# Scores of a tile held back until the first-layer product of the tile four places before it is placed, with the order drawn anew

## The chip, the cores and the metric

The kernel runs on one core of a Trainium2 chip. The metric is the time of one execution in device microseconds (us). The core has a matrix engine (PE), a vector engine (DVE), an activation engine (ACT), a general engine (POOL), and a sync engine (SP) that issues all DMAs of this kernel. Each engine works through its own list of instructions in order; an instruction waits until the semaphores it names are reached, and everything behind it on the same engine waits with it.

## The reference, cut to what matters

Attention with pooled keys and values, then two feed-forward layers over its output:

```python
k_p = k.reshape(B, H, Sp, 8, D).mean(axis=3)       # B, H, S, D = 8, 8, 576, 64; Sp = 72
v_p = v.reshape(B, H, Sp, 8, D).mean(axis=3)
scores = q @ k_p.T / sqrt(D)
attn = softmax(scores)                             # over the 72 pooled keys
x = (attn @ v_p) as (4608, 512)
h = x @ w_in                                       # 512 -> 1024
solu = h * softmax(h)
ln = layernorm(solu) * g_ln
y = ln @ w_out                                     # 1024 -> 512
h2 = y @ w2_in                                     # 512 -> 2048
out = (h2 * sigmoid(1.702 * h2)) @ w2_out          # 2048 -> 512
```

## The kernel before, in words

The program has two parts. The first, up to about 450 us, computes attention and the first feed-forward layer and also prepares the weights of the second layer. The second, up to the end, is the second layer, written out by hand (lines 1300 to 1700). The change touches the first part alone.

The 4608 tokens are 36 tiles of 128, and every tile goes through one strand of steps (`attention`, line 854):

- its scores on PE (buffer `psx`, one bank pair for all tiles), taken from the transposed query `qt` and the pooled keys `kbd`;
- maximum and difference on DVE (`mx`, `e`), exponent on ACT, sum on DVE (`rs`), division on POOL (`e<-e,rs`), then a split into two 16-bit halves on ACT and POOL (`st`);
- a DMA transpose on SP (`aT<-st`), from tile 4 on issued for two tiles together;
- the values product on PE (buffer `psv`, a single one; `aT` with `vst`), which ACT and DVE copy out as `xT`.

A second strand (`hidden`) does the first-layer product of the tile on PE: 24 matmuls into `psh` (two buffers) from `xT` and the weights `w1i`, then maximum (`hmx`) and the softmax-times-h (`tt`) on DVE with an exponent on ACT (`he`). `hid[t]` is set when the plan gives the tile its `psh` buffer, before its matmuls are placed. A third strand per pair of tiles (`norm`) normalises on POOL and ACT (`zs`), transposes by DMA (`zT<-zs`), and starts two halves of the second matrix (`project`): each is 2 x 24 matmuls into `psy` (a single buffer) from `zT` and `w1o`.

Other strands pool keys and values of the eight batches (`half` to `kp`, `vp`; for batches 1 and 2 with matmuls into `psy`), and bring in and split the weights (`raw`, `w_f`, `hi`, `lo`). Each scale of a weight or of the values needs the largest value over all partitions: a matmul of `diag` with `ones` into `psy` (early) or `psv` (later), read by DVE (`w1o_all`, `w2all`, `v_all`). Until DVE has read it, that buffer is taken.

The order is made at build time by `Plan` (line 198). It keeps a list of strands, estimates for the next step of each when it could start, adds a term for its due time and a random number (`DRAWS`: up to a time of the plan's own clock, a size, a seed), and emits the step with the lowest score. What comes out is a fixed list for every engine. A lambda that a strand yields is a condition on the plan: the strand offers no further step until it holds. It puts no semaphore into the program; it only moves what is emitted. In the order rows, a name such as `psx_1467` is a buffer with the running number it got in that build, so numbers differ between the two kernels.

Of the kernel before, what the change touches and what calls it, by code (L numbers as in the profile page):

```python
# [78 lines left out]
DNS = 7  # L79
SG = 4  # L80
LAST = 90000
LATE = 3000
LATE_TURN = 3000
TTS = 4
DRAWS = ((70e3, 600, 13), (200e3, 150, 4), (330e3, 150, 13), (1e9, 150, 1))
V_TOP = 2.0 ** 14

TOP3 = 2.0 ** -29 * (1 - 2.0 ** -23)
# [95 lines left out]
class Plan:  # L184
# [7 lines left out]
    def __init__(self):  # L192
        self.free = dict.fromkeys(("pe", "dve", "act", "pool", "sp", "dma", "none"), 0.0)
        self.uses, self.floor, self.rings, self.ring_of = {}, {}, {}, {}
        self.strands, self.now, self.warm, self.pool_from = [], None, 0.0, 0.0
        self.draws = [(until, size, random.Random(seed)) for until, size, seed in DRAWS]

    def start(self, steps, due):
        s = Strand(self, steps, due)
        self.strands.append(s)  # L200
        return s
# [42 lines left out]
    def take(self, op, t, engine):  # L244
        if engine == "sp":
            begin = max(self.free["dma"], t + (1275 if op.turn else 1100))
            self.free["dma"] = end = begin + op.cost["sp"]
            self.free["sp"] = max(t + 625, end - 920) if op.turn else t + 520
            end += LATE_TURN if op.turn else LATE
            engine = "dma"  # L250
# [46 lines left out]
def moe_kernel(ctx: ExitStack, tc: tile.TileContext, qT, kT, vT, w_in, w_out, g_ln, w2_in, w2_out, eye, outT):  # L297
# [138 lines left out]
    with ExitStack() as ph:  # L436
# [22 lines left out]
        def until(*strands):  # L459
            return lambda: all(s.ended for s in strands)  # L460

        def there(*ins):

            return Op(("none",), lambda engine: None, [], ins, {"none": 0})
# [296 lines left out]
        def spans(t):  # L761

            b0, s0 = divmod(t * P, S)
            n = min(P, S - s0)
            parts = [(0, n, b0)]
            if n < P:
                parts.append((n, P - n, b0 + 1))
            return parts
# [88 lines left out]
        def attention(t):  # L857
# [5 lines left out]
            if t < 2:  # L863
                tiles[t].due = max(due(t) + LAG_ATT, DUE_ATT + STEP_ATT * t)
            yield lambda: all(k_ready[b] for _, _, b in spans(t)) and (t == 0 or scored[t - 1])
            e = yield New(sb, [P, H, SP], F32, "e", bufs=2)
            yield there(qt, *(kbd[b % 2] for _, _, b in spans(t)))
            ps = yield New(psx, [P, 2, 512], F32, "psx", "psx")
# [211 lines left out]

        EARLY, LATE = (slice(0, 2), slice(3, 6)), (slice(2, NS, 4),)

        class Quarter:
# [22 lines left out]
            def run(self, due):  # L1106
# [22 lines left out]
                def combine(slot, a, b, how):  # L1129
                    return VG("tensor_tensor", out=w[:, slot], in0=w[:, a], in1=w[:, b], op=how)  # L1130
# [4 lines left out]
                def split(slots):  # L1135
                    for s in slots:
                        yield A(out=hi[:, s], in_=w[:, s], func=AF.Copy)
                    for s in slots:
                        yield VG("tensor_tensor", out=lo[:, s], in0=w[:, s], in1=hi[:, s], op=ALU.subtract)
# [5 lines left out]
                yield combine(6, 1, 5, ALU.subtract)  # L1145
                second = start(split(LATE), due)
                yield until(first, second)
# [16 lines left out]
        def factors():  # L1164
            yield until(*units)
            cw, top = s1("cw", NU), s1("top")
            yield V(
                "scalar_tensor_tensor", out=co, in0=w1o_dn, scalar=1.0 / LN_UP, in1=g_dn, op0=ALU.mult, op1=ALU.mult
            )
            yield V("tensor_scalar_mul", ch, w2i_dn, co)  # L1170
            yield V("tensor_mul", cw, ch, w2o_dn)
            yield V("tensor_reduce", out=top, in_=cw, axis=AX.X, op=ALU.max)
            yield V("tensor_scalar_mul", co, top, 1.0 / G_DOWN)
            yield V("reciprocal", top, co)
            yield V("tensor_scalar_mul", gu, w2o_dn, top)

        def prepare_second():
# [46 lines left out]
            ytmp.release()  # L1224
            start(first_unit(), due(NTILE) + LAST)
            yield lambda: pairs[-1].normed
# [3 lines left out]
        def first_unit():  # L1230

            def product(p, bank, again=False):
                rows = [
                    (bank, w2i[0][:, w, A_OF[p], k], tok.ys[:, i, B_OF[p], k], False, k == 1 and w == 1)
                    for k in range(2)
                    for w, i in PASSES
                ]
                if again:
                    return T([(*r, True) for r in rows])
                return T([(*rows[0][:3], True, False)] + rows[1:])  # L1240

            def snap(i, bank):
                return A(out=first_c[:, i], in_=bank, func=AF.Copy)

            def add(i, bank):
                return V("tensor_tensor", out=first_c[:, i], in0=bank, in1=first_c[:, i], op=ALU.add)

            yield lambda: scored[NTILE - 1] and hid[NTILE - 1]
            banks = []
            for pool, name, bufs in ((psx, "psx", 1), (psh, "psh", 2), (psh, "psh", 2)):  # L1250
                banks.append((yield New(pool, [P, 2, 512], F32, name, name, bufs)))
            a, b, d = (x[:, 0, :TH] for x in banks)
            yield product(1, a)
            yield snap(Q11, a)
            yield product(2, b)
            yield add(Q11, b)
            yield product(6, a, True)
            yield snap(Q12, a)
            yield product(3, b)
            yield add(Q12, b)  # L1260
            yield product(7, a, True)
            yield snap(Q22, a)
            yield product(5, d)
            yield add(Q22, d)
            yield add(Q12, d)
            yield product(4, a, True)
            yield snap(Q21, a)
            drop(*banks)
# [3 lines left out]
        q_loaded, scored, turned, valued, hid = ([False] * NTILE for _ in range(5))  # L1272
# [21 lines left out]
        def due(t):  # L1294
            return FIRST_STEP + STEP * t
# [12 lines left out]
        user(keys(0, DUE_K0), DUE_K0)  # L1308
        user(eye_load(), DUE_W_IN + 1e3)
        tiles = [start(attention(t), DUE_Q + 100 * t) for t in range(2)]  # L1310
        am_in = s1("w1i_am", KM)
        w_in_done = user(w_in_scale(), DUE_SCALE)
# [4 lines left out]
        for b in range(1, B):  # L1317
            d = due(b * S // P + LEAD_KV) if b > 1 else DUE_KV1
            user(keys(b, d), d)
            user(values(b, d), d)  # L1320
        tiles += [start(attention(t), max(due(t) + LAG_ATT, DUE_ATT + STEP_ATT * t)) for t in range(2, NTILE)]
        pairs = [Pair(i) for i in range(NTILE // 2)]
        for p in pairs:
# [22 lines left out]
        factors_done = start(factors(), due(NTILE))  # L1346
        start(prepare_second(), due(NTILE) + LAST)
        plan.run()
# [381 lines left out]
```

## Time and profile before

| | us |
|---|---|
| median of 3 runs | 1172.87 |
| lowest, highest | 1170.4, 1172.99 |
| profiled execution, time | 1172.71 |
| profiled execution, span of its instructions | 1170.8 |
| PE busy | 1123.7 (96%) |
| ACT, DVE, POOL busy | 753.6, 727.7, 616.9 |

The profile is of one execution. Busy time of an engine counts its arithmetic instructions; the span runs from the first instruction to the last. A row of the timeline gives the start in us from the start of the span, the length, the engine, line and operation, what is written from what, and in brackets the idle time of the engine just before with the engine and buffer that ended it. PEclk is the granted clock of PE as a share of its full 2.4 GHz.

### The profile page before, as it was taken

What the parts mean: (1) busy time and instruction counts of PE and PEld (TensorE: products, weight loads), DVE (VectorE), ACT (ScalarE), POOL (GpSimd) and SP (SyncE); (2) the same over time, 40 slices, a digit from 0 to 9 for tenths busy, and PEclk for the clock granted to TensorE, in tenths of its full rate; (3) what the DMA queues carried; (4) which work ended last, traced back from release to release, by engine and by line L of the source; (5) the groups of instructions that cost most, each with busy time, mean ns of one, the idle gap of its engine ahead of it and who ended that gap; (6) DMA issues with size and microseconds to landing.
All of it is one profiled execution on the core that took longest, in us unless ns stands there. A gap on an engine that the chain in (4) does not pass through costs nothing.

```text
span 1170.8 us, 19698 instructions
## 1 busy us (share of the span) xinstructions
PE 1123.7 (96%) x7737; PEld 724.8 (62%) x7737; DVE 727.7 (62%) x1106; ACT 753.6 (64%) x997; POOL 616.9 (53%) x643
## 2 busy tenths in 40 slices
PE   4878999999999999999999999999999999999998
PEld 3545666667676667775566666666665665566665
DVE  7998888777677753337653774567266636753650
ACT  6888997988898784647624762674367337624740
POOL 4466999989999885325503530461056016503530
PEclk9999999999999999999999999999999999999999
DMA  9969999999999679255465355536453653463131
GB/s 366 276 179 286 226 274 286 285 260 247 287 272 216 162 181 268 74 174 235 138 197 183 127 165 163 190 125 203 141 174 126 214 167 137 147 203 117 60 120 60
DMA packets 247356, 225.75 MB, mean 193 GB/s; under 512 B 165728, under 2 KB 218080, under 8 KB 246752
## 3 DMA queue, kind: packets, MB, share of 16 engines
q1 hardware_dynamic: 247264, 224.50, 66.4%
q8 instruction: 60, 0.98, 0.3%
q14 instruction: 32, 0.26, 0.1%
HBM read 151.06 MB, written 33.55 MB: 158 GB/s over the span
## 4 chain that ended last, share of the span: by engine, by line
PE 70%; POOL 14%; ACT 7%; DVE 5%; issue 3%; DMA 1%; SPq 0%; POOLq 0%; ACTq 0%; DVEq 0%
PE bank_a L1386 32%; PE bank_d L1386 16%; PE bank_b L1386 8%; PE psy L537 6%; PE psh L537 6%; POOL w_f L496 4%; POOL lo L496 3%; PE psv L537 2%; POOL zs L496 2%; POOL st L496 2%; POOL e L496 1%; POOL q L496 1%; PE psx L537 1%; ACT st L496 1%; ACT tt L496 1%
## 5 line engine op out<-in xcount | busy, mean ns | idle before, releaser
L1386 PEld LDWEIGHTS <-w2o 128*128 128x128 f16 x2016 | 197.0, 98 | 130.4
L1386 PEld LDWEIGHTS <-w2i 128*128 128x128 f16 x1974 | 193.1, 98 | 128.4 <-issue 1.0
L349 POOL TENSOR_TENSOR w_g<-w_g 128x384 f32<-128x384 f32 x42 | 45.9, 1093 | 397.6 <-ACT w_g L1465 397.6
L1480 DVE SCALAR_TENSOR_TENSOR g<-w_g,gu_b,g 128x1152 f16<-128x1152 f32 (+1 forms) x96 | 175.9, 1833 | 87.1 <-ACT g L1475 86.8
L537 PE MATMUL psh<-w1i,xT 128*128 128x512 f16 x864 | 200.7, 383 | 5.5 <-ACT xT L496 3.8
L1386 PE MATMUL bank_a<-ys,w2i 128*128 128x384 f16 x1128 | 205.3, 326 | 0.0
L1386 PE MATMUL bank_a<-g,w2o 128*128 128x384 f16 x1152 | 201.6, 326 | 0.0
L537 PEld LDWEIGHTS <-w1o 128*128 128x128 f16 x1728 | 168.9, 98 | 32.1 <-DMA zT<-zs 2.9
L537 PE MATMUL psy<-zT,w1o 128*128 128x256 f16 x1536 | 177.9, 274 | 3.8 <-DMA zT<-zs 2.4
L1475 ACT ACTIVATE g<-w_g,gu_b 128x1152 f16<-128x1152 f32 (+1 forms) x96 | 134.1, 1409 | 48.5 <-POOL w_g L352 37.6
L1405 ACT ACTIVATE c<-bank_a 128x384 f32<-128x384 f32 x188 | 90.6, 482 | 102.3 <-PE bank_a L1386 101.8
L537 PEld LDWEIGHTS <-xT 128*128 128x128 f16 x864 | 82.9, 98 | 97.5 <-issue 4.9
L1386 PE MATMUL bank_d<-g,w2o 128*128 128x384 f16 x576 | 104.2, 326 | 0.0
L496 POOL TENSOR_TENSOR zs<-tt,zs 128x1024 f16<-128x1024 f32 x36 | 78.4, 2177 | 43.7 <-ACT zs L496 43.3
L1386 PE MATMUL bank_d<-ys,w2i 128*128 128x384 f16 x564 | 101.1, 326 | 0.0
L1465 ACT ACTIVATE w_g<-c,ch_b 128x1536 f32<-128x1536 f32 x47 | 73.7, 1568 | 28.3 <-DVE c L1408 28.3
L352 POOL TENSOR_TENSOR w_g<-w_g 128x384 f32<-128x384 f32 x42 | 82.5, 1963 | 0.0
L1408 DVE SCALAR_TENSOR_TENSOR c<-bank_d,c 128x384 f32<-128x384 f32 x94 | 51.9, 552 | 44.2 <-ACT c L1405 29.5
L496 POOL TENSOR_TENSOR lo<-w_f,hi 128x512 f16<-128x512 f32 (+1 forms) x48 | 64.8, 1369 | 6.8 <-DMA w2i_dram<-lo 5.2
L496 DVE TENSOR_REDUCE hmx<-psh 128x1 f32<-128x1024 f32 x36 | 43.8, 1218 | 35.1 <-PE psh L537 34.9
L537 PE MATMUL psx<-kbd,qt 128*128 128x144 f32 (+1 forms) x320 | 46.2, 306 | 13.9 <-ACT kbd L496 9.8
L496 DVE CUSTOM_DVE_ANT_0 tt<-psh,he 128x1024 f32<-128x1024 f32 x36 | 43.8, 1217 | 23.7 <-ACT he L496 21.8
(205 smaller groups left out, 1606.7 us busy)
## 6 DMA issues: line engine op xcount, KB each, us to landing
w2i<-w2i_dram SPq DMA_DIRECT2D x48, 896.0 KB, 4.5
w2o<-w2o_dram SPq DMA_DIRECT2D x84, 512.0 KB, 3.7
half<-kT SPq DMA_DIRECT2D x16, 576.0 KB, 6.3
half<-vT SPq DMA_DIRECT2D x16, 576.0 KB, 5.9
qt<-qT SPq DMA_DIRECT2D x36, 256.0 KB, 4.2
y_dram<-y SPq DMA_DIRECT2D x36, 256.0 KB, 3.5
y<-y_dram SPq DMA_DIRECT2D x48, 192.0 KB, 4.1
raw<-w_in SPq DMA_DIRECT2D x16, 512.0 KB, 7.8
```

Of the source, the lines that this page charges most:

```text
L349: eng.tensor_tensor(out=w[:, 1], in0=q[:, Q12], in1=q[:, Q11], op=ALU.subtract)
L352: eng.tensor_tensor(out=w[:, 3], in0=q[:, Q21], in1=w[:, 2], op=ALU.subtract)
L496: getattr(eng, name)(*args, **kw)
L537: nc.tensor.matmul(*p[:3], start=p[3], stop=p[4], skip_group_check=len(p) > 5)
L1386: nc.tensor.matmul(bank, self.weight(p, kk, w), self.data(p, kk, i), start=(first and kk == 0 and w == 0 and i == 0), stop=(last and kk == ...
L1405: nc.scalar.activation(out=self.c[:, i], in_=getattr(self, bank), func=AF.Copy, scale=self.scale)
L1408: nc.vector.scalar_tensor_tensor(out=self.c[:, i], in0=getattr(self, bank), scalar=self.scale, in1=self.c[:, i], op0=ALU.mult, op1=ALU.add,)
L1465: nc.scalar.activation(out=self.w[:, 0:4], in_=self.c, func=AF.Gelu_apprx_sigmoid, scale=self.ch)
L1475: nc.scalar.activation(out=self.g[s.start][:, 0], in_=self.w[:, s], func=AF.Copy, scale=self.gu)
L1480: nc.vector.scalar_tensor_tensor(out=self.g[s.start][:, 1], in0=self.w[:, s], scalar=self.gu, in1=self.g[s.start][:, 0], op0=ALU.mult, op1 ...
```

## The change

Two things change. A condition is put ahead of the scores of a tile: from tile 4 on, they are not offered to the plan until the first-layer product of the tile four places back has its buffer (`AHEAD_TO = 99` lies beyond the last tile, so the condition holds for all). And the table of random draws is another one: three stretches in place of four, with other seeds and other ends. Both move instructions in the lists of all engines in the first part; no operation of the reference is added or dropped. Between the engines that can each do a step, a few steps change place: PE has the same 14,804 rows, with 48 `project` matmuls in `psy` that were in `psv`; 8 exponents of one tile go to ACT, head by head.

```diff
 LAST = 90000
+AHEAD = 4
+AHEAD_TO = 99
 LATE = 3000
 LATE_TURN = 3000
 TTS = 4
-DRAWS = ((70e3, 600, 13), (200e3, 150, 4), (330e3, 150, 13), (1e9, 150, 1))
+DRAWS = ((70000.0, 600, 3), (360000.0, 150, 3), (1000000000.0, 150, 174017))
...
             yield lambda: all(k_ready[b] for _, _, b in spans(t)) and (t == 0 or scored[t - 1])
+            yield lambda: t < AHEAD or hid[t - AHEAD] or t >= AHEAD_TO
             e = yield New(sb, [P, H, SP], F32, "e", bufs=2)
```

SP, the stretch where the first normalised pair (`zs`, `zT`) meets the first loads of `w2_in` (`raw`). Before:

```order
42 L528 DMA raw_896<-w2_in 128x4x256 x2
43 L528 DMA raw_897<-w2_in 128x4x256 x2
44 L528 DMA raw_894<-w2_in 128x4x256 x2
45 L528 DMA qt_966<-qT 128x512
46 L528 DMA raw_895<-w2_in 128x4x256 x2
47 L528 DMA_TRANSPOSE zT_862<-zs_887 128x16x128
48 L528 DMA_TRANSPOSE zT_862<-zs_951 128x16x128
49 L528 DMA_TRANSPOSE aT_958<-st0_135 128x16x128
50 L528 DMA_TRANSPOSE aT_1053<-st1_136 128x16x128
```

The same stretch of SP now:

```order
42 L530 DMA raw_879<-w2_in 128x4x256 x2
43 L530 DMA half_877<-kT 128x1152
44 L530 DMA raw_942<-w2_in 128x4x256 x2
45 L530 DMA_TRANSPOSE zT_868<-zs_870 128x16x128
46 L530 DMA_TRANSPOSE zT_868<-zs_899 128x16x128
47 L530 DMA qt_1008<-qT 128x512
48 L530 DMA raw_940<-w2_in 128x4x256 x2
49 L530 DMA raw_941<-w2_in 128x4x256 x2
50 L530 DMA_TRANSPOSE aT_1000<-st0_135 128x16x128
51 L530 DMA_TRANSPOSE aT_1053<-st1_136 128x16x128
```

The two transposes of the first pair stood behind four pairs of `w2_in` loads and stand behind two; the transposes of tiles 6 and 7 (`aT`) stay behind all four.

DVE, around the values products of tiles 6 and 7 (`xT<-psv`). Before:

```order
171 L496 TENSOR_REDUCE w2a1_147<-w2am_146 128x1
172 L496 SCALAR_TENSOR_TENSOR xT_1234<-psv_1204,xT_1234 128x512
173 L496 TENSOR_REDUCE mx_1251<-psx_1246 128x8
174 L496 TENSOR_TENSOR e_1245<-psx_1246,mx_1251 128x576
175 L496 ISA tt_1275,mean_955<-psh_1047,he_1176 128x1024
176 L496 ISA mean_955 128x1
177 L496 SCALAR_TENSOR_TENSOR xT_1271<-psv_1238,xT_1271 128x512
```

Now:

```order
171 L498 TENSOR_REDUCE w2am_146<-raw_941 128x1
172 L498 TENSOR_REDUCE w2am_146<-raw_942 128x1
173 L498 TENSOR_REDUCE w2all_145<-psv_1222 128x1
174 L498 TENSOR_SCALAR w2all_145<-w2all_145 128x1
175 L498 ISA tt_1221,mean_951<-psh_1032,he_1212 128x1024
176 L498 ISA mean_951 128x1
177 L498 SCALAR_TENSOR_TENSOR xT_1244<-psv_1227,xT_1244 128x512
```

A scale product (`w2all`) now uses `psv` just ahead of tile 6, and DVE reads it behind two measurements of loaded weights. On PE the scores of tile 10 stood between the two values products; now the two stand next to each other.

PE, the scores of tile 12. Before:

```order
884 L537 MATMUL psh_1317<-w1i0_127,xT_1271 128x512
885 L537 MATMUL psx_1467<-kbd0_133,qt_1252 128x144 x4
886 L537 LDWEIGHTS xT_1271
887 L537 MATMUL psh_1317<-w1i0_127,xT_1271 128x512
888 L537 LDWEIGHTS xT_1271
```

Now:

```order
1067 L539 LDWEIGHTS vst0_131
1068 L539 MATMUL psv_1602<-aT_1286,vst0_131 64x128
1069 L539 MATMUL psx_1611<-kbd0_133,qt_1298 128x144 x4
1070 L539 LDWEIGHTS xT_1564
1071 L539 MATMUL psh_1609<-w1i0_127,xT_1564 128x512
```

They stood inside the first-layer product of tile 7 (`psh_1317`) and now stand right ahead of that of tile 8 (`psh_1609`), the tile four places back. In the other direction, the values products of tiles 12 to 15 come earlier: that of tile 12 stood behind the first-layer product of tile 11 and now stands inside that of tile 10.

## Rows read from the trace of the kernel before

**Rows 1.** Windows: length, busy us by engine, clock, DMA share, GB/s.

```profile
0.00:112.00 112.00, 80.27 (x562) 56.53 (x564) 94.91 (x179) 89.05 (x128) 62.42 (x73) 0.95 0.93 277
112.00:420.00 308.00, 297.31 (x2434) 207.49 (x2429) 233.72 (x433) 269.21 (x397) 286.02 (x340) 1.00 1.02 248
```

**Rows 2.** Waits of PE: buffer, releaser, total us, times, longest.

```profile
PE psv L537 <- DVE xT L496: 7.2, 8, 2.0
PE psy L537 <- ACT kp L496: 5.3, 2, 2.9
```

**Rows 3.** Timeline of PE, first values and first-layer products.

```profile
30.05 0.64 PE L537 MATMUL psv<-aT,vst 128*64 128x128 f16 x16
...
35.70 2.74 PE L537 MATMUL psh<-w1i,xT 128*128 128x512 f16 x6 [3.83 <-ACT xT L496]
```

**Rows 4.** Timeline of PE, two scale products at 70 us.

```profile
70.30 0.22 PE L537 MATMUL psy<-diag,ones 128*128 128x128 bf16 x1 [2.85 <-ACT kp L496]
72.54 0.22 PE L537 MATMUL psy<-diag,ones 128*128 128x128 bf16 x1 [2.03 <-DVE mean L496]
```

**Rows 5.** Timeline of PE, tiles 4 to 7 and first project half.

```profile
84.45 0.69 PE L537 MATMUL psv<-aT,vst 128*64 128x64 f16 x32
85.08 1.25 PE L537 MATMUL psx<-kbd,qt 128*128 128x144 f32 x8
87.57 0.64 PE L537 MATMUL psv<-aT,vst 128*64 128x128 f16 x16 [1.24 <-DVE xT L496]
88.14 5.35 PE L537 MATMUL psh<-w1i,xT 128*128 128x512 f16 x24
...
102.63 7.08 PE L537 MATMUL psy<-zT,w1o 128*128 128x256 f16 x48 [2.37 <-DMA zT<-zs]
109.64 0.64 PE L537 MATMUL psv<-aT,vst 128*64 128x128 f16 x16
...
111.69 0.64 PE L537 MATMUL psv<-aT,vst 128*64 128x128 f16 x16 [0.23 <-DVE xT L496]
```

**Rows 6.** Windows around the wait for zT.

```profile
99.90:103.40 3.50, 1.13 (x9) 0.70 (x8) 3.47 (x11) 3.48 (x6) 1.15 (x1) 1.00 1.04 232
103.40:106.80 3.40, 3.40 (x18) 2.35 (x16) 3.20 (x9) 3.37 (x5) 2.35 (x2) 0.50 1.21 222
```

**Rows 7.** Timeline of SP, w2_in loads and transposes.

```profile
80.80 5.28 SPq L528 DMA_DIRECT2D raw<-w_in  x6
...
90.78 9.57 SPq L528 DMA_TRANSPOSE zT<-zs  x2
```

**Rows 8.** Timeline of POOL, second tile of the first pair.

```profile
90.00 2.14 POOL L496 TENSOR_TENSOR zs<-tt,zs 128x1024 f16<-128x1024 f32 x1 [1.30 <-ACT zs L496]
```

**Rows 9.** Timeline of PE, later waits for psv.

```profile
187.87 0.70 PE L537 MATMUL psv<-aT,vst 128*64 128x64 f16 x32 [1.10 <-DVE xT L496]
...
206.74 0.64 PE L537 MATMUL psv<-aT,vst 128*64 128x128 f16 x16 [1.25 <-DVE v_all L496]
...
305.34 0.69 PE L537 MATMUL psv<-aT,vst 128*64 128x64 f16 x32 [2.10 <-DVE w2all L496]
...
401.68 0.69 PE L537 MATMUL psv<-aT,vst 128*64 128x64 f16 x32 [1.96 <-DVE xT L496]
```

**Rows 10.** Timeline of PE, project and scores in the steady stretch.

```profile
118.49 2.78 PE L537 MATMUL psy<-zT,w1o 128*128 128x256 f16 x24
...
126.32 1.14 PE L537 MATMUL psx<-kbd,qt 128*128 128x144 f32 x8
```

**Rows 11.** Timeline of POOL, end of tiles 8 and 34.

```profile
108.67 1.29 POOL L496 TENSOR_TENSOR st<-e,st 128x576 f16<-128x576 f32 x1
...
425.55 1.27 POOL L496 TENSOR_TENSOR st<-e,st 128x576 f16<-128x576 f32 x1
```

**Rows 12.** Transposes aT on SP from 90 to 420 us.

```profile
DMA to landing us min/median/max: 3.8/5.0/11.1
```

**Rows 13.** Timeline of PE, scores of tile 34.

```profile
402.31 1.25 PE L537 MATMUL psx<-kbd,qt 128*128 128x144 f32 x8
```

## The prediction

> **What bounds the kernel now.** I read the windows first, then the waits of PE, then its timeline at each long wait, and last the engines that ended those waits. In the steady stretch PE is busy 297.3 of 308 us, and POOL 286.0 of 308 [rows 1]. PE does the same products in either order, so all that a new order can give is PE's idle time: 112 - 80.3 = 31.7 us in the first 112 us, 308 - 297.3 = 10.7 us in the steady stretch, and some 1.7 us where PE ran at half its clock behind a wait (below). The hand-written second part, from about 510 us, keeps its lists in substance; I cost it at nothing.
>
> The idle time ahead of 112 us is mostly filling: the first keys, the first weights. In the steady stretch the reader is to see that PE waits hardly anywhere but at `psv`, the single buffer that a values product needs and that DVE has to read out first: 7.2 us over 8 waits for `xT`, some of them early, and the long single ones at 187.87, 206.74, 305.34 and 401.68 us [rows 2, 9]. So the question is which hand-overs of `psv` and `psy` get more PE work between them, which get less, and whether the held-back scores make the attention of a tile late.
>
> **The change part by part.** The sum goes against the profiled execution, 1172.71 us (span 1170.8 and 1.9 around it; the median of the runs is 1172.87).
>
> Start. The first values product ran at 30.05 us and the first-layer product at 35.70, after 3.83 us of idle time that ACT's copy of `xT` ended [rows 3]. Now the scale of `w_in` comes earlier in the lists, since its product no longer stands behind the 16 pooling matmuls of batch 1, but the transpose of tile 0 comes later, since POOL does two weight multiplications ahead of it instead of one, and 8 more pooling matmuls move into the gap. I take 0; at best the whole 3.8 us go, at worst the later transpose costs 3.
>
> The scales near 70 us. Two products of `diag` wait in turn for ACT's copy of `kp` (2.85 us) and for DVE (2.03 us), both because `psy` is taken [rows 4]. The first of the two, of `g_ln`, is now emitted earlier; but right behind the other, of `w_out`, stand four pooling matmuls that want `psy` again and so wait for the same DVE reading. I take 0, bounds 0 and -2.0.
>
> Tiles 4 and 5. Between their values products stood the scores of tile 8, and PE still waited 1.24 us [rows 5]. They now follow each other at once: the wait becomes 87.57 - (84.45 + 0.69) = 2.4 us, and the scores are done later. +1.2 us, bounds 0 and +1.3.
>
> First projection. PE waited 2.37 us for `zT`, and its clock then stood at 0.50 (1.2 GHz) from 103.4 to 106.8 us; the 48 matmuls took 7.08 us, where two runs of 24 later take 2.62 each from start to start, 118.49 to 121.11, the row of 24 itself 2.78 with its overlap [rows 5, 6, 10]. The transposes of this pair held SP for 9.57 us from 90.78, though POOL was done with the second tile at 92.14: they were queued behind four pairs of `w2_in` loads [rows 7, 8]. Now they stand ahead of two of these four, and ACT and POOL come to the second `zs` some 3 us earlier, counting the work ahead of it. The data can be there near 96 us, PE arrives at about 100.3. So the wait goes, 2.4 us, and the slow clock with it, 7.08 - 2 x 2.7 = 1.7 us: -4.1 us, bounds 0 and -4.1.
>
> By the Trainium skill, page "TensorE: Matmul & The Clock Gate", section "HAM oscillation — how this bites in real kernels", a wait for data in front of a product lets the clock fall, so that the product starts cold each time. The trace agrees at 102.63 us, with 0.50 behind 2.37 us of waiting, but not at 305.34, where 2.10 us of waiting left the clock at 1.00 in the window of the steady stretch [rows 1, 6, 9]. If each new wait of the list below cost a cold start like that one, the sum would be some 2 to 5 us higher.
>
> Tiles 6 and 7. Behind that projection a scale product now takes `psv` immediately ahead of tile 6, and DVE reads it only behind two measurements of `raw` weights, the last of the four loads. And tile 7 follows tile 6 with nothing between, where the scores of tile 10 hid all but 0.23 us of a hand-over of 111.69 - (109.64 + 0.57) = 1.5 us [rows 5]. I take 1.2 for the first and 1.2 more for the second, +2.4 us; bounds 0 and +5, the upper one if the last load is late.
>
> The steady stretch. Of the long waits, those for tile 13 (1.10 us), 14 (1.25), 22 (2.10) and 31 (1.96) have now 24 to 72 more project or first-layer matmuls ahead of them; what is late on DVE there hides behind these, 2.6 us and more [rows 9, 10]. -6.4 us, bounds -10.7 (all idle time of the stretch) and 0. New thin places: tiles 11 and 19 follow 10 and 18 with 6 first-layer matmuls between, 1.3 us against a hand-over of 1.5; tiles 16 and 17 lie closer; a scale product stands just ahead of tiles 10, 18, 26 and 30; and a 1.3 us stretch lies between two projections that share `psy`. With half a microsecond to one each, +4.0 us, bounds 0 and +14 (seven places with the longest wait seen, 2.1).
>
> The condition itself adds no wait on the chip. It shortens the stretch between scores and values product: counted on PE from the lists, from 35 to 56 us (tiles 8 to 35) to 28 to 49. What has to fit in: scores to the end of `st`, 109.96 - 85.08 = 24.9 us for tile 8 and 426.82 - 402.31 = 24.5 for tile 34 (first and last of 27 tiles, from 14 to 46, middle 22) [rows 5, 11, 13]; then the transpose, 5.0 us in the middle, 11.1 at most [rows 12]. That is 27 in the middle. Tile 12 is the tightest: between its scores and its values product now stand 60 first-layer matmuls (2.5 x 5.35), 96 project matmuls (4 x 2.62), three scores (3.4) and little else, 28 us [rows 5, 10]. I have put 1 us of lateness for it into the +4.0.
>
> Sum: 0 + 0 + 1.2 - 4.1 + 2.4 - 6.4 + 4.0 = -2.9 us, or 1169.8. DVE and ACT, which carry the moved steps, are idle for 74 and 39 us of the steady stretch [rows 1]; that is the cover of all that I cost at nothing, and where it fails, a wait of 1 to 2 us appears.
>
> **The rivals.**
>
> *The attention comes late (slower).* If scores to `st` keeps taking as long as for the slower tiles, 25.8 us (the value that three of the 27 exceed) and more with POOL at 93%, and the transpose takes 7, a values product needs 33 us. Tiles 12, 15, 24, 33 and 34 leave 28 to 31. They lie at three places; each would cost 3 to 4 us, +10.5 in all, and PE waits at `psv` for the DMA of `aT`. It decides from 28 us on. For it: POOL's rows in line, transposes held up by bulk loads [rows 7, 12]. Against it: the earlier scores just waited longer for buffers, so part of the 22 us was queueing behind other tiles. 1169.8 + 10.5 = 1180.
>
> *Nothing gained.* The projection's gain of 4.1 stays, but thin hand-overs cost all that the removed waits give, 6.4, and tiles 4 to 7 cost 3.6: 1172.2. For it: DVE's list sets these waits, and it is about as busy in any order.
>
> *More gained.* The plan sees hand-overs of `psy` and `psv` and places the reading on DVE right behind; then the thin places cost only 1 us in place of 4.0, and tiles 4 to 7 cost 1.6 in place of 3.6. 1172.7 - 4.1 - 6.4 + 1 + 1.6 = 1164.8. For it: 8 of the waits of `psv` average under 1 us [rows 2].
>
> *The condition does nothing* by itself, the redraw all: the plan would already hold scores back by its buffers. From tile 12 on, scores are placed 2 to 15 us of PE work later than before, so it acts; I keep it out of the chances.
>
> **How the numbers follow.** My forecast has 0.36 (1166 to 1173), late attention 0.21, nothing gained 0.19, more gained 0.24. About 0.3%, 3.5 us, is what a measurement of this kernel tells from no change. The forecast lies 2.9 us below, so it falls to faster by 0.16, to same by 0.18 and to slower by 0.02; nothing gained gives 0.15 to same, 0.04 to slower; late attention goes to slower, more gained to faster. Faster 0.40, same 0.33, slower 0.27. The range takes in the better half of the late attention and most of what more could be gained: 1162 to 1178.
>
> **What would show it.** In the profile after: no wait for `zT` at the first projection and a clock of 1.00 from 100 to 110 us; waits of 2 us and of over 1 us for `psv` at tiles 5 and 7, near 87 and 108 us; the wait near 70 us still there; in the steady stretch other tiles waiting at `psv`, ended by DVE, of some 8 us in all (10.7 idle now, less 6.4, plus 4.0). A wait for the DMA `aT<-st` at a values product of 2 us or more, above all at tiles 12, 24 or 33, would prove the forecast wrong and the first rival right; an idle time of PE ahead of 112 us that differs by over 4 us from 31.7 would put the cause in the start, which I costed at nothing.

## The result, and the profile after

The changed kernel takes 1183.95 us in the median of 6 runs (1181.85 to 1187.27), the kernel before on the same chip 1172.82 us (1170.03 to 1175.31): a ratio of 1.0107, with a 95% interval of 1.0090 to 1.0124. It is slower by 11.1 us between the medians and by some 12.5 us by the ratio, where 2.9 us less were forecast, and it lies above the range. The profiled execution took 1182.62 us, its span is 1180.8 us, 10.0 us longer than before.

The windows of the kernel after, with the columns of [rows 1] (length, then busy us of PE, PEld, DVE, ACT, POOL, the clock, the DMA share, GB/s):

```profile
0.00:112.00 112.00, 78.26 (x564) 55.33 (x565) 96.42 (x190) 91.60 (x132) 67.26 (x79) 0.95 0.99 274
112.00:420.00 308.00, 294.20 (x2359) 202.59 (x2358) 220.69 (x409) 263.15 (x386) 277.95 (x331) 0.98 1.04 245
```

PE idles for 33.7 us ahead of 112 us (31.7 before) and for 13.8 us in the steady stretch (10.7 before), and in that stretch its mean clock is 0.98 in place of 1.00. Busy time hides what a slow clock costs, so I set the two traces side by side at equal work: the work ahead of a matmul, each kind of matmul counted at its spacing at full clock, is taken from the time at which the matmul starts. What is left is all that PE has lost until then, in us:

| PE work done | before | after | difference |
|---|---|---|---|
| 88 | 41.1 | 41.8 | +0.7 |
| 96 | 41.7 | 49.2 | +7.5 |
| 184 | 46.6 | 49.8 | +3.2 |
| 240 | 47.6 | 60.8 | +13.2 |
| 352 | 53.3 | 60.8 | +7.5 |
| 432 | 53.7 | 61.2 | +7.5 |
| 464 | 55.3 | 65.3 | +10.0 |

So the front (to some 130 us of time) comes out even. Between the jumps the order before loses more than the new one, by 4.3 us from 96 to 184 and by 5.7 from 240 to 352; the four waits that were to go lie in these stretches. Three jumps, called hits from here on, take 6.8, 10.0 and 2.5 us. The first two are in the waits of PE from 112 to 450 us (buffer, releaser, total us, times, longest), which answer to [rows 2]:

```profile
PE psv L539 <- DMA half<-kT: 4.3, 1, 4.3
PE psh L539 <- DVE mean L498: 3.6, 1, 3.6
PE psy L539 <- ACT y L498: 2.3, 4, 1.3
PE psv L539 <- DVE xT L498: 2.0, 1, 2.0
PE psv L539 <- DVE v_all L498: 1.5, 1, 1.5
```

The first hit is at tile 8. PE's timeline (start, duration, in brackets the idle time ahead and its releaser), and DVE's of the same stretch:

```profile
129.50 0.22 PE L539 MATMUL psv<-diag,ones 128*128 128x128 bf16 x1
129.77 2.56 PE L539 MATMUL psy<-zT,w1o 128*128 128x256 f16 x22
136.67 1.06 PE L539 MATMUL psv<-aT,vst 128*64 128x128 f16 x16 [4.33 <-DMA half<-kT]
137.66 5.20 PE L539 MATMUL psy<-zT,w1o 128*128 128x256 f16 x24
```

```profile
129.89 1.23 DVE L498 CUSTOM_DVE_ANT_0 tt<-psh,he 128x1024 f32<-128x1024 f32 x1 [2.51 <-ACT he L498]
...
133.82 1.22 DVE L498 TENSOR_REDUCE w2am<-raw 128x1 f32<-128x1024 f32 x1 [2.50 <-DMA raw<-w_in]
134.95 1.22 DVE L498 TENSOR_REDUCE hmx<-psh 128x1 f32<-128x1024 f32 x1
...
136.33 0.28 DVE L498 TENSOR_REDUCE w2all<-psv 128x1 f32<-128x128 f32 x1
```

The page names the transfer `half<-kT` as what ended PE's wait, but nothing that the values product needs comes from there. DVE's row does: `psv` held a scale product, and its reader `w2all` ended at 136.33 + 0.28 = 136.61. The product was there at 129.72, but its reader stood in DVE's list behind `w2am`, which waited for its load until 133.82, and behind `hmx`. Behind the wait 24 project matmuls took 5.20 us in place of 2.62.

The second hit is a group of four waits from 256 to 296 us, on PE; then DVE ahead of the last of them, and SP ahead of that:

```profile
257.51 0.64 PE L539 MATMUL psv<-aT,vst 128*64 128x128 f16 x16 [1.47 <-DVE v_all L498]
...
272.71 2.78 PE L539 MATMUL psy<-zT,w1o 128*128 128x256 f16 x24 [1.27 <-ACT y L498]
...
287.26 0.64 PE L539 MATMUL psv<-aT,vst 128*64 128x128 f16 x16 [2.00 <-DVE xT L498]
...
295.21 7.03 PE L539 MATMUL psh<-w1i,xT 128*128 128x512 f16 x24 [3.64 <-DVE mean L498]
```

```profile
292.57 1.35 DVE L498 TENSOR_REDUCE kp<-half 128x144 f32<-128x1152 f32 x1 [5.25 <-DMA half<-kT]
293.84 1.22 DVE L498 CUSTOM_DVE_ANT_0 tt<-psh,he 128x1024 f32<-128x1024 f32 x1
```

```profile
274.77 9.84 SPq L530 DMA_TRANSPOSE zT<-zs  x2
...
286.79 0.41 SPq L530 DMA_DIRECT2D half<-kT  x1
```

The load left SP at 286.79, behind a pair of transposes that had held SP for 9.84 us, and landed at 292.57; the reader that frees `psh` (`tt`) stood behind its reader. The third hit is at 510.38, on PE and ahead of it on ACT, which comes to `c_kept` only behind `ys` and a table load:

```profile
510.38 1.24 PE L539 MATMUL psx<-ys,w2i 128*128 128x384 f16 x6 [2.09 <-ACT c_kept L498]
511.41 2.13 PE L539 MATMUL psh<-ys,w2i 128*128 128x384 f16 x6
```

```profile
506.87 1.57 ACT L498 ACTIVATE ys<-w_y,y_up 128x1536 f16<-128x1536 f32 x1
508.45 1.28 ACT L498 ACT_TABLE_LOAD   x1
...
509.86 0.47 ACT L498 ACTIVATE c_kept<-psx 128x384 f32<-128x384 f32 x1
```

The clock, in the five windows at half speed (columns as above):

```profile
70.96:74.37 3.41, 3.41 (x12) 1.86 (x11) 3.19 (x14) 2.90 (x5) 3.33 (x3) 0.50 0.87 190
84.60:91.40 6.80, 4.73 (x27) 3.10 (x27) 5.34 (x10) 6.54 (x12) 4.57 (x3) 0.50 1.10 290
...
135.80:142.60 6.80, 5.93 (x40) 4.27 (x39) 4.02 (x14) 2.92 (x4) 6.64 (x8) 0.50 1.15 191
296.20:299.70 3.50, 3.50 (x10) 1.18 (x8) 3.40 (x7) 2.49 (x5) 3.50 (x3) 0.51 1.23 237
511.30:514.70 3.40, 3.40 (x15) 1.91 (x13) 0.56 (x1) 0.49 (x1) 0.00 (x0) 0.50 0.02 5
```

Each of the three hits is followed by one; the first two stand in the front. The places of the front, which answer to [rows 4, 5]:

```profile
68.85 0.22 PE L539 MATMUL psy<-diag,ones 128*128 128x128 bf16 x1 [1.62 <-ACT kp L498]
70.08 1.48 PE L539 MATMUL psy<-half,eye_t 128*128 128x144 f32 x8 [1.02 <-DVE w1o_all L498]
...
86.00 1.07 PE L539 MATMUL psv<-aT,vst 128*64 128x128 f16 x16 [3.26 <-DVE xT L498]
...
101.92 5.40 PE L539 MATMUL psy<-zT,w1o 128*128 128x256 f16 x48
...
108.65 0.64 PE L539 MATMUL psv<-aT,vst 128*64 128x128 f16 x16 [1.12 <-DVE w2all L498]
110.76 0.64 PE L539 MATMUL psv<-aT,vst 128*64 128x128 f16 x16 [1.48 <-DVE pw L498]
```

### The profile page after: what moved, and what is told of

Its sections match the earlier page's. It is cut to its first block, busy times and chain, and to the rows that moved or that the text cites. A ratio compares the mean times of both kernels' runs of the same rounds, so it can differ in the third digit from the quotient of the medians.

```text
span 1180.8 us, 19743 instructions
## 1 busy us (share of the span) xinstructions
PE 1127.2 (95%) x7737; PEld 725.3 (61%) x7737; DVE 721.4 (61%) x1106; ACT 756.6 (64%) x1004; POOL 616.2 (52%) x642
## 4 chain that ended last, share of the span: by engine, by line
PE 78%; POOL 8%; ACT 5%; DVE 3%; DMA 3%; issue 2%; SPq 0%; POOLq 0%; DVEq 0%; ACTq 0%
PE bank_a L1389 31%; PE bank_d L1389 16%; PE psy L539 10%; PE psh L539 9%; PE bank_b L1389 8%; PE psv L539 2%; PE psx L539 2%; POOL w_f L498 2%; DMA half<-kT 2%; POOL zs L498 1%; POOL st L498 1%; POOL lo L498 1%; POOL e L498 1%; ACT he L498 1%; DMA raw<-w_out 1%
## 5 line engine op out<-in xcount | busy, mean ns | idle before, releaser
L539 PE MATMUL psy<-zT,w1o 128*128 128x256 f16 x1584 | 185.2, 275 | 2.3 <-ACT y L498 2.3
L498 POOL TENSOR_TENSOR lo<-w_f,hi 128x512 f16<-128x512 f32 (+1 forms) x46 | 61.9, 1356 | 10.1 <-DMA w2i_dram<-lo 7.1
L539 PE MATMUL psx<-kbd,qt 128*128 128x144 f32 (+1 forms) x320 | 46.6, 307 | 14.9 <-ACT kbd L498 11.2
```

The lines of the kernel that those rows point to most:

```text
L498: getattr(eng, name)(*args, **kw)
L539: nc.tensor.matmul(*p[:3], start=p[3], stop=p[4], skip_group_check=len(p) > 5)
```

## Experiments

The first theory was that DVE's list stands at loads that land late, wherever the draw puts them; its first rival that the condition itself costs. The expectations number those that came later. All ratios are against the kernel before, timed beside it on the same chip; 0.1% is 1.2 us. The changed kernel stands at 1.0107.

### Is it the condition or the order drawn anew?

**e1**, the condition with the old draws.

```diff
-DRAWS = ((70000.0, 600, 3), (360000.0, 150, 3), (1000000000.0, 150, 174017))
+DRAWS = ((70e3, 600, 13), (200e3, 150, 4), (330e3, 150, 13), (1e9, 150, 1))
```

> The condition on the scores, with the draws of the kernel before. Late loads (theory 1: what costs in the kernel after is DVE's list standing at a step whose load has not landed, with the reader of psv or psh behind it; where that falls is an accident of the draw): the condition by itself costs little, 1168 to 1178 us, and no wait of PE over 3 us between 120 and 300 us that ends on DVE. Scores held back (theory 2: the condition makes attention late and bunches DVE's work): 1179 us or more, with waits of PE like those of the kernel after in sum (about 15 us at psv, psh and psy between 112 and 320 us) in whatever places.

**e2**, the new draws without the condition.

```diff
-AHEAD = 4
+AHEAD = 99
```

> The new draws without the condition. Late loads: the order is a third one from tile 5 on, so the time is one more draw, 1168 to 1184 us, and where it is above 1177 there stands a step of DVE that waits 2.5 us or more for a load, with the reader that PE waits for behind it. Scores held back: without the condition the loss is gone, 1168 to 1175 us.

**e4**, the condition with other seeds.

```diff
-... (360000.0, 150, 3), (1000000000.0, 150, 174017))
+... (360000.0, 150, 5), (1000000000.0, 150, 5))
```

> The kernel after, condition included, with other seeds of the second and third stretch (5 and 5 for 3 and 174017). Late loads: the hits fall elsewhere, and their sum scatters by some 8 us from draw to draw: 1170 to 1186 us. Scores held back: the same loss in another order, 1181 to 1187 us.

**e5**, the kernel before with other seeds.

```diff
-DRAWS = ((70e3, 600, 13), (200e3, 150, 4), (330e3, 150, 13), (1e9, 150, 1))
+DRAWS = ((70e3, 600, 13), (200e3, 150, 5), (330e3, 150, 14), (1e9, 150, 2))
```

> The kernel before, without the condition, with other seeds from the second stretch on (5, 14, 2 for 4, 13, 1). Lucky draw (theory 3: the order before was an uncommonly good draw, and any other, with the condition or without, costs about 10 us): 1178 to 1188 us. Condition (theory 2: the condition is what costs): 1168 to 1176 us.

**e13**, the condition with the seeds of e5, and **e14**, the seeds of e4 with `AHEAD = 99`.

> The condition on the scores with the seeds that gave 1182.1 us without it. The draw alone costs, the condition nothing or little: 1178 to 1187 us, a third kernel with the condition among the other draws without it. The condition costs of itself: 1186 us or more, as with the draws of the kernel before (1188.7 us).

> The seeds that gave 1182.7 us with the condition, without it. The draw alone: 1178 to 1187 us. The condition costs of itself: 1173 to 1179 us.

Measured:

| draws of | without the condition | with it |
|---|---|---|
| before | 1 | e1: 1188.68 us, 1.0139 [1.0110, 1.0168] |
| after | e2: 1183.12, 1.0089 [1.0061, 1.0116] | 1183.95, 1.0107 [1.0090, 1.0124] |
| e4 | e14: 1185.21, 1.0125 [1.0099, 1.0151] | e4: 1182.74, 1.0082 [1.0055, 1.0108] |
| e5 | e5: 1182.07, 1.0104 [1.0082, 1.0126] | e13: 1186.19, 1.0131 [1.0105, 1.0156] |

Every other order of this table is slower than that of the kernel before, by 0.8 to 1.4%, with the condition or without. Of the three pairs beside the old draws two are faster without it and one with it, by 0.2 to 0.4%. So the condition has no effect that these runs show beyond the order that it redraws; the order drawn anew has. The expectation of 1168 to 1178 us for e1 was wrong: with the old draws the condition also makes a new order, and e1's time would by itself have spoken for the rival. It is e2, as slow without the condition, that speaks against it. e13 lies where its two expectations meet and decides nothing alone.

**e15** and **e16** ask which stretch the kernel before owes its time to.

```diff
-... (330e3, 150, 13), (1e9, 150, 1))
+... (330e3, 150, 13), (1e9, 150, 2))
```

```diff
-... (330e3, 150, 13), (1e9, 150, 1))
+... (330e3, 150, 14), (1e9, 150, 1))
```

> The kernel before with another seed in its last stretch alone (2 for 1), so that its order is the same until about 330 us. If the redraw costs stretch by stretch (the other draws lost 8 to 10 us more than the kernel before between 85 and 470 us of the product's work, 2 to 5 of them behind 330 us): 1173 to 1177 us. If the good order stands or falls as a whole: 1180 us or more. If the kernel before is no better than others there: 1169 to 1173 us.

> The kernel before with another seed in its third stretch (14 for 13), so that its order is the same until about 200 us and another from there on. Stretch by stretch: 1175 to 1181 us, more than with the last stretch alone. As a whole: 1180 us or more. No better than others there: 1169 to 1173 us.

e15, whose order differs from 348 us on, took 1171.87 us, 1.0007 [0.9990, 1.0023]: against this one other draw the last stretch is no better. e16, whose order differs from 211 us on, took 1187.33 us, 1.0133 [1.0107, 1.0159], more than the stretch-by-stretch theory gave. That does not place what the old order has over the others. By lost time the seven redrawn kernels of the table lose some 3 to 7 us more than the kernel before between 122 and 195 us already, and more than half of what e16 loses comes behind 325 us. (One execution shows this to some 3 us: e15 had lost up to 3 us more than the kernel before where their order is the same.) The advantage of the old order is spread over the stretch from 122 us on.

The largest hit of e16 has nothing to do with loads. PE, DVE and POOL there:

```profile
243.03 1.06 PE L537 MATMUL psv<-aT,vst 128*64 128x128 f16 x16 [6.29 <-DVE xT L496]
```

```profile
232.28 8.97 DVE L496 SCALAR_TENSOR_TENSOR raw<-raw 128x1024 int32<-128x1024 int32 x1
241.17 1.21 DVE L496 TENSOR_REDUCE hmx<-psh 128x1 f32<-128x1024 f32 x1
242.31 0.67 DVE L496 SCALAR_TENSOR_TENSOR xT<-psv,xT 128x512 f16<-128x512 f32 x1
```

```profile
231.02 3.87 POOL L496 TENSOR_TENSOR lo<-w_f,hi 128x512 f16<-128x512 f32 x3
234.85 2.13 POOL L496 TENSOR_TENSOR zs<-tt,zs 128x1024 f16<-128x1024 f32 x1
236.94 1.15 POOL L496 TENSOR_TENSOR e<-e,rs 128x576 f32<-128x576 f32 x1
238.05 2.12 POOL L496 TENSOR_TENSOR zs<-tt,zs 128x1024 f16<-128x1024 f32 x1
```

DVE's `raw` takes 1.34 us in the middle of 22 in the kernel before:

```profile
L496 DVE SCALAR_TENSOR_TENSOR raw<-raw x22: 1215/1337/2252, 25.7 to 403.0; 128x1024 int32<-128x1024 int32 x22
```

Here it took 8.97 us and ended 1.1 us behind the last of a run of POOL operations without a gap.

### Do the named hits make the difference?

**e3** moves seven DVE steps, first readers of loads, a few places back in the order of the kernel after.

```diff
+MOVES = {630: 654, 1243: 1258, 1290: 1309, 1373: 1397, 1375: 1397, 1384: 1397, 1408: 1450}
...
-            s.item.emit(engine)
+            if n in MOVES:
+                held.append((MOVES[n], s.item.emit, engine))
+            else:
+                s.item.emit(engine)
```

> The kernel after with only seven DVE steps moved, all of them first readers of a load (w2am<-raw near 134 and 256 us, kp<-half near 266.6 and 292.6, vp<-half twice and vam near 281 to 284), each to a place some steps later, behind the reader of psv or psh; nothing moves on any other engine. Late loads: PE's wait of 4.33 us that ends near 136.7 falls under 1.5 us and the half clock of 135.8 to 142.6 us is gone, the waits of 1.47, 1.27, 2.00 and 3.64 us between 256 and 296 us fall to 3 us in sum and the half clock of 296 to 299.7 us is gone; 6 to 11 us less, 1173 to 1178 us. Scores held back: PE waits at the same places for the same time, since the work behind is late anyway, 1182 to 1186 us.

It took 1182.81 us, 1.0087 [1.0063, 1.0112]: the gain of 6 to 11 us did not come, though the time is the one that the rival gave. The first hit went as expected, which the rival did not give, and by the table of lost time e3 was 7.0 us ahead of the kernel after at a work of 96 and 4.9 at 240, but 1.2 behind at 304. PE in e3:

```profile
132.24 0.64 PE L548 MATMUL psv<-aT,vst 128*64 128x128 f16 x16 [0.22 <-DVE w2all L507]
...
286.02 0.94 PE L548 MATMUL psv<-aT,vst 128*64 128x128 f16 x16 [3.58 <-DVE xT L507]
...
306.73 2.45 PE L548 MATMUL psy<-zT,w1o 128*128 128x256 f16 x21 [1.81 <-ACT y L507]
...
361.62 0.64 PE L548 MATMUL psv<-aT,vst 128*64 128x128 f16 x16 [2.29 <-DVE xT L507]
```

The wait of 3.58 us goes back over ACT to POOL, and on POOL to a store that had to land before `lo` could be written again:

```profile
266.56 1.16 POOL L507 TENSOR_TENSOR lo<-w_f,hi 128x512 f16<-128x512 f32 x1 [4.17 <-DMA w2i_dram<-lo]
```

```profile
280.40 1.16 ACT L507 ACTIVATE st<-e 128x1152 f16<-128x1152 f32 x1 [3.42 <-POOL e L507]
...
284.66 0.57 ACT L507 ACTIVATE xT<-psv 128x512 f16<-128x512 f32 x1
```

**e17** adds the tail: two products of the first unit behind a projection that is ready. The moves of e3 stay, and the table of moves has four more:

```diff
+... 2324: 2332, 2325: 2332, 2326: 2332, 2330: 2332}
```

> The kernel after with the seven DVE steps moved as before and, at the end of the first part, the second pair of the first unit's products held behind the last but one projection, which is ready (PE's wait of 2.09 us near 510 us for c_kept, with the half clock that follows it in the kernel after). Hits are local (theory 1): the tail's 2 us go for good, 1179 to 1181.5 us. Given back: 1182 to 1184 us.

The wait of 2.09 us and its half clock are gone, but the time is 1183.76 us, 1.0114 [1.0087, 1.0141], no different from e3's: not shown in the time.

### Which engine has no slack?

Three kernels with the order of the kernel after and one more operation for each tile: **e6** has the first of these added lines, **e7** the second, **e8** the third. The lines that set up what they write are left out here.

```diff
             x_turned[t] = xT
+            nc.sync.dma_start(probe_d[t], qT[t][:, 0:2])
+            nc.gpsimd.tensor_tensor(out=probe[:, 0:128], in0=probe[:, 0:128], in1=probe[:, 128:256], op=ALU.add)
+            nc.vector.tensor_tensor(out=probe, in0=probe, in1=probe, op=ALU.add)
```

> The kernel after with one more transfer for each of the 36 tiles, 128 KB from qT to a place in memory that nobody reads, issued on SP behind the tile's xT; the order of all else is the same. At the 262 GB/s of the stretch from 112 to 320 us each is worth 0.5 us of the queues, 18 us in all. No slack (theory 4: the transfers, whose queues show a busy share above 1.0 from 80 to 370 us, or POOL, busy for 94 to 98% in 152 to 232 and 320 to 370 us, carry the pace of that stretch, and PE's waits are what is left over of it): 6 us or more on top of 1184 us, 1190 to 1202 us. Only blocked list heads (theory 1): up to 3 us more, 1183 to 1187 us.

> The kernel after with one more POOL operation for each of the 36 tiles (128x128 f32 on a scratch tile that nobody reads; estimated at 0.45 us from 0.73 us for 128x256 and 0.19 us for 128x2, so 16 us in all); the order of all else is the same. No slack on POOL: 6 us or more on top of 1184 us, 1190 to 1200 us. POOL has slack: up to 3 us more.

> The kernel after with one more DVE operation for each of the 36 tiles (128x256 f32 on a scratch tile; about 0.35 us each from 0.76 us for 128x576, 13 us in all), behind xT. DVE is busy for 75% of the time from 112 to 320 us: if theory 4 is right in naming POOL and the transfers alone, 0 to 3 us more, 1184 to 1187 us; if DVE's list is as tight as POOL's, 5 us or more, 1189 us and above.

e6: 1194.49 us, 1.0205 [1.0180, 1.0230]. e7: 1188.78 us, 1.0163 [1.0123, 1.0203]. e8: 1191.84 us, 1.0188 [1.0158, 1.0218]. Against 1.0107 that is 11.5, 6.6 and 9.5 us: each addition costs time. For e7 the intervals just touch, and its time lies between its two forecasts. e8's is above what the theory of POOL and transfers alone gave. But DVE's probes were longer than estimated, 37.4 us in all in place of 13:

```profile
L958 DVE TENSOR_TENSOR probe<-probe x36: 404/846/4515, 38.8 to 471.8; 128x256 f32<-128x256 f32 x36
```

So e8 does not show DVE to be as tight as the others. Nor is it shown that the cost comes by DVE's own list: the longest probe, 4.5 us at 216.34, ran beside POOL operations for 4.3 us of it, and what the probes keep from POOL was not tried apart.

Now less work in place of more, in both orders. These kernels leave out part of the computation, and their output is another. **e9** (order of after) and **e10** (of before) load a quarter of `qT` for the tiles from 4 on,

```diff
-            yield D(qt, qT[t])
+            load = D(qt, qT[t])
+            if t >= 4:
+                load.emit = lambda engine: nc.sync.dma_start(qt[:, 0:1], qT[t][:, 0:1])
+            yield load
...
-                        qt[:, p, o : o + n],
+                        qt[:, p if t < 4 else 0, o : o + n],
```

and **e11** (after) and **e12** (before) have a copy in place of a subtraction, 0.61 us in place of 1.16 at the median.

```diff
-                        yield VG("tensor_tensor", out=lo[:, s], in0=w[:, s], in1=hi[:, s], op=ALU.subtract)
+                        low = VG("tensor_tensor", out=lo[:, s], in0=w[:, s], in1=hi[:, s], op=ALU.subtract)
+                        low.emit = copy(lo[:, s], hi[:, s])
+                        yield low
```

> The kernel after in the same order, with 64 KB of qT loaded in place of 256 KB for tiles 4 to 35 (their scores are computed from the first quarter of qT four times over, so the output is another): 6.3 MB less, 24 us of the queues at the 262 GB/s of the stretch from 112 to 320 us. Transfers set the pace (theory 4, narrowed: the price that the added transfers showed, 10.5 us for 18 us of queues, holds downwards too, because loads and stores land earlier and the lists of DVE and POOL stand less): 8 to 14 us less, 1170 to 1176 us, and DVE's waits for half and raw from 112 to 320 us fall from 20 us to under 10. The order itself (theory 5: the lists wait for each other in this order however fast the transfers are): 0 to 4 us less, 1180 to 1184 us.

> The kernel before with the same shorter loads of qT. Transfers set the pace, and a draw is good or bad by how it lives with late ones: before has less to win than after, 2 to 7 us less, 1165 to 1170 us, and the two kernels stand 3 to 7 us apart in place of 12. The order itself: 0 to 4 us less, and the two stand 10 to 14 us apart.

> The kernel after in the same order, with the 48 subtractions of lo (POOL, 65 us in all) replaced by a copy of hi into lo (the low parts of the second layer's weights are wrong by that); an estimate of 20 to 35 us less work on POOL, from 1.16 us for 128x512 and no row for the copy. At the price that the added POOL work showed (5 us for 20 us): 5 to 9 us less, 1175 to 1179 us. POOL not the pace, only in the way now and then: 0 to 4 us less.

> The kernel before with the same copies. If a fuller POOL is what separates the two orders, they stand 3 to 7 us apart (before 1 to 5 us less, 1167 to 1171 us); if not, both gain alike and stand 10 to 14 us apart.

| | order of after | order of before | apart |
|---|---|---|---|
| as it is | 1.0107 | 1 | 1.07% |
| shorter loads | e9: 1177.26 us, 1.0048 [1.0029, 1.0066] | e10: 1166.94 us, 0.9963 [0.9948, 0.9979] | 0.85% |
| less POOL work | e11: 1184.53 us, 1.0119 [1.0082, 1.0157] | e12: 1167.26 us, 0.9963 [0.9951, 0.9975] | 1.56% |

With lighter transfers the first hit stays and the second is gone from e9 (no wait of 1.2 us or more between 136 and 499 us) and does not come back: lost time at work 352 is 51.7 us in place of 60.8. DVE's waits for `half` and `raw` from 112 to 320 us fall from 20.1 to 6.3 us:

```profile
DVE kp L498 <- DMA half<-kT: 2.2, 1, 2.2
DVE w2am L498 <- DMA raw<-w_in: 2.0, 1, 2.0
DVE vp L498 <- DMA half<-vT: 1.1, 1, 1.1
```

So late transfers do make the second hit. But the order of before gains as well, and the two stay 0.85% apart, 10 us, where 3 to 7 us were expected. Less POOL work brings the order of before 0.37% and the order of after nothing that shows (its interval is 0.4% wide to either side); a fuller POOL is not what parts them.

**e18** has the moves of e17 and the loads of e9.

> The same moves and the shorter loads of qT for tiles 4 to 35 (output another, as there) in one kernel. If the three hits near 134, 255 to 300 and 510 us are what separates the two orders, once the transfers no longer bring the second one back: 1168 to 1172 us, and not more than 5 us above the kernel before with the same shorter loads (1166.9 us). If the order is slower in ways that the hits only show: 1174 us or more.

1174.69 us, 1.0026 [1.0009, 1.0044]: of 1.07% all three remedies take 0.81, but against e10, which has the shorter loads in the order of before, 0.63% stays, 7 us. The three hits are gone or down to 1.7 us in its trace, and its lost time grows all the same from 43.0 (work 80) to 58.9 us (work 464), where e10 goes from 38.6 to 48.0: 4.4 us of the distance are there at a work of 80, and 6.5 come behind. The pieces are smaller; the longest wait of PE from 112 to 520 us is 1.94 us, for `aT` at 195.52, with half a clock behind it.

No kernel here with the whole computation is faster than the kernel before.

## Why the prediction was wrong

**The step that failed** is that of the new thin places in the steady stretch: "With half a microsecond to one each, +4.0 us, bounds 0 and +14". New waits from 130 us to the end of the first part took 6.8 + 10.0 + 2.5 = 19.3 us, with the half clock behind them; 16.8 of these lie in the steady stretch, above the bound, and the 2.5 near 510 us, where I cost everything at nothing. I had sized the places by the number of hand-overs with little PE work between, at the waits of the order before. Of the hits only tile 18, 1.47 us at 257.51, was on that list. What decides is what stands ahead of the reader in the list of its own engine, and when that can go: a load on DVE in the kernel after, a run of POOL's in e16. I had looked at this at tile 6, two measurements of `raw` ahead of the scale's reader, and at no other of the places where it recurs. I took the 74 us for which DVE was idle as cover; an idle engine whose list stands at a load covers nothing.

**The level of the forecast.** I summed differences at named places as if all else stayed level. The eight orders drawn anew from 200 us or earlier, that of the kernel after among them, lie 0.8 to 1.4% above the old one, so an order drawn anew starts at +10 to +16 us, and the places that I could name are less than half of it: mending three of them, with lighter transfers in both orders, left 7 us of 12. That the old order might be an exception was none of my rivals.

**Removed waits**: 6.4 us forecast, and at the four tiles named PE no longer waits at all. The stretches around them give 4.3 + 5.7 = 10.0 us, near the bound of 10.7; the 3.6 beyond the four waits are other losses of the order before, which I had not named. Right in kind.

**The front**, forecast -0.5, came to +0.7. First projection -4.1: right, no wait for `zT` and 48 matmuls in 5.40 us. Tiles 6 and 7 +2.4: right, 1.12 + 1.48 - 0.23 = 2.4. Scales near 70 us, 0: the two waits went from 4.88 to 2.64 us, just past the bound of -2.0. Tiles 4 and 5, +1.2: the wait is 3.26 us, 2.0 more than before, and half a clock for 4.73 us of work adds 2.4. The bound of 1.3 was too small. Start, 0: what is left of the front, 0.7 + 4.1 - 2.4 + 2.2 - 4.4 = +0.2.

**The clock.** The Trainium skill, page "TensorE: Matmul & The Clock Gate", section "HAM oscillation — how this bites in real kernels", says that a wait for data makes the next product start cold. The trace agrees behind the long waits: those of 3.26, 4.33, 3.64 and 2.09 us have the half clock behind them, and so has the pair of 1.62 and 1.02 us at 68.85 and 70.08; that of 2.00 us at 287.26 starts none. The prediction priced this at 2 to 5 us if it held for each new wait. The five windows hold 21.0 us of PE's busy time, so half speed cost 10.5 us there, an estimate. The prediction had named one such stretch in the order before, 1.7 us; its trace has three (from 35.1, 72.7 and 103.4 us, 9.7 us of busy time), 4.8 us by the same estimate. That is 5.7 us more in the new order, where PE's whole busy time is 3.5 us longer for the same products. Behind the three hits it is 6.4 of their 19.3 us.

**The rivals.** The attention was not late: no wait of PE for `aT` anywhere in the trace after, and no effect of the condition in the three pairs of draws beside the old ones. In other kernels such waits do stand, of 2.2 us at most, with the condition (e6, e9, e18) and without (e2, e14). "The condition does nothing by itself, the redraw all", which I kept out of the chances, comes nearest. "Nothing gained" named thin hand-overs that cost what the removed waits give, 6.4 us: it had new waits for the loss, at a third of the size and mostly at places where PE did not wait.

**Still open** is why the order before loses so little from 122 us on. Whether its seeds had been picked by their time, which would make any redraw a loss, is not on record here. The orders redrawn have their hits from different causes (loads at the head of DVE's list, stores at POOL's, POOL's runs ahead of a DVE step), and no one remedy closes the gap.

## What to carry to other kernels

When a change redraws a whole order, time a few other draws of the old rules before reading anything into the change: here the draw was worth 0.8 to 1.4% and the rule nothing that shows. To price a new wait, read the list of the engine that ends it, not the gap on the engine that waits: what stands ahead of the reader, and does it wait for a load. And a wait that is mended in one place can come back a little later, as in e3; follow the lost time to the end of the stretch.

## What was not expected of the hardware

A DVE operation on two operands in SBUF took 8.97 us in e16, in place of 1.34, and ended only once a run of POOL operations without a gap was over. e8's small DVE operations took 404 ns at least, 846 in the middle and 4515 at most. The Trainium skill, page "SBUF — State Buffer", section "SBUF: two separate sides", says that such DVE operations and POOL share a pair of ports, and that the one that comes second is blocked. The trace of e16 agrees, and shows more in this one case: DVE was not let in between the POOL instructions that followed each other from 232.28 to 240.17 us.

A wait of 2.09 us at the same product left the half clock behind in the kernel after (510.38), where the next two groups of six took 1.24 and 2.13 us, and not in e3, where they took 1.14 us each.

The same order waits differently from one execution to the next: at the product that waited 1.25 us for `v_all` in [rows 9], e15, whose order is the same to there, waited 3.20 us.
